# First four weight units loaded and converted along attention steps 28 to 84, in rooms of their own

## The chip, the cores and the metric

One core of one Trainium2 chip. The time is that of one execution on the device, in microseconds (us); of several runs the median is given. TensorE is called PE, VectorE DVE, ScalarE ACT, GpSimd POOL; SP issues the transfers.

## What is computed

Attention with two mixings over heads (2 batches, 12 heads, 448 rows, head size 64), then two dense blocks on the 896 rows of width 768. The reference, cut:

```python
scores = scale * q @ k.T
scores = einsum("bhij,hg->bgij", scores, w_pre)      # mix the heads
attn = softmax(scores)                               # maximum, exp, sum
attn = einsum("bhij,hg->bgij", attn, w_post)         # mix again
x = attn @ v                                         # rows of 768
xn = x / sqrt(mean(x * x) + 1e-6) * rms_g
y = (silu(xn @ w_gate) * (xn @ w_val)) @ w_out       # 768 -> 1536 -> 768
out = elu(y @ w_in) @ w_out2                         # 768 -> 2048 -> 768
```

The weights of the dense blocks arrive as 64-bit floats.

## The kernel before

**Weight units.** The weights are cut into units of 128 x 768 numbers. Units 0 to 23 are w_gate and w_val in turn, 0.77 MB each. `load_w` (L206) brings one into the tile raw (two rooms). `convert` (L214) makes it usable in stages: rebase (ACT L229 reads the high words into w32, DVE L232 shifts the low words), sign (DVE L237 clips and finds the largest number of each row, DVE L245 sets the sign), join (DVE L251 puts both words together and, for every second unit, L270 prepares the pair's largest numbers). For a pair of such units bound (PE L277) and factor (DVE L284, L288, L290) make a scale; then scaled (six ACT L301), high16 (ACT L305) and low16 (DVE L309) split the unit in two 16-bit halves in a tile whl (three rooms). `load_to(n)` issues all loads below n; `next_convert` and `next_scaled` hand out the first and the second part of the stages.

**Attention.** `attention` (L370) first turns q and k of batch 0 and splits each in two parts (par). There are twelve such parts a batch, but nine rooms of their own; `parts_of` (L431) gives three of batch 0 the rooms of whl, and of batch 1 the rooms of raw to two and of whl to one. The scores are written to memory (s_d) and come back in groups of ten rows by twelve heads (sg). There are 90 groups, and the main loop (L834) works as a pipeline with one group a step: at step t PE mixes group t+1 (L544, or L547 to L549), DVE takes the maximum of group t (L556), ACT the exponential (L564), DVE makes the low part el of group t-2 (L602) and the high part eh of t-1 (L595, or ACT L593), PE mixes group t-3 again (L623, it reads eh and el), ACT copies it out (L635). Beside that hq holds the turning of batch 1's q and k and the score rows, some a step. After each window of some 60 to 70 rows the products with v run (L659) and a chain of ten small stages follows, one a step: L665 and squares on POOL, mean (L681), root (POOL L692), diagonal (L696), spread (PE L702), normed (L705), high (ACT L711), low (L714) into xhl, which the dense blocks read.

**What sets the order.** All is recorded by hand in program order; each engine works in that order. In the loop one entry of the list tail is taken at the end of a step when hq is empty: load units 0 and 1, convert unit 0, load 2, convert 1, load 3, scale 0, scale 1. From the last step on `fill` also takes products of the first two units on batch 0's rows (`first_gate`, 12 pieces of three products) between the chain's stages, and with each an entry of more: convert units 2 and 3, load 4 and 5, scale 2. `run` (L909) then works unit by unit: unit 0 on batch 1's rows begins with the first L202 that reads the last window's xhl, and for u = 0 it also scales unit 3.

In this section step t is the t-th of the 90 rows of L556, counted from 0.

## Time and profile before

| | us |
|---|---|
| median of 3 runs | 782.35 (781.74 to 783.04) |
| the profiled execution | 782.59, its span 780.9 |
| PE busy | 747.8 (96%) |
| DVE busy | 552.1 (71%) |
| ACT busy | 438.5 (56%) |
| POOL busy | 94.6 (12%) |
| L556 of steps 28, 60, 67, 74, 84 | at 109.26, 191.53, 209.80, 227.25, 255.28 |
| first L202 on the last window's rows | at 292.58 |

How to read it: up to some 80 us attention starts up; from there to 270 us the 90 steps run; the dense blocks follow and fill PE to the end. The busy share of PE says where it waits for others, and the granted clock how fast it ran: 1.00 stands for 2.4 GHz, and the other level is 1.2 GHz. An idle DVE or ACT costs nothing unless PE waits for it in the end.

### The profile page before, as it was taken

Reading aid. Unit: us, or ns where it says so; the run is one execution under the profiler, and the core shown is the slowest. Engines: PE = TensorE matmul, PEld = TensorE weight load, DVE = VectorE, ACT = ScalarE, POOL = GpSimd, SP = SyncE. Lnnn points to the kernel's source line nnn. Section 1 sums busy time; section 2 is a strip of 40 time slices with the busy share of each in tenths; the row PEclk is TensorE's granted clock in tenths of the full one; section 3 lists DMA queues with packets and bytes.
Section 4 is the critical chain, followed back from the end, with each engine's and each line's share of the span. In section 5 each row is a group of like instructions: output and inputs, shape, how many; then the busy total and the mean of one; then the engine's idle time right before and its main releaser. Section 6 shows DMA issues by size and latency. Waiting matters only on the chain.

```text
span 780.9 us, 14563 instructions
## 1 busy us (share of the span) xinstructions
PE 747.8 (96%) x5683; PEld 590.3 (76%) x5683; DVE 552.1 (71%) x1101; ACT 438.5 (56%) x910; POOL 94.6 (12%) x117
## 2 busy tenths in 40 slices
PE   7789999999998879999999999999999999999996
PEld 5446787777776654555555589999999999999996
DVE  4358997788899867878878766653888788643731
ACT  3478788878777845666576622322776665221310
POOL 0122344334445300000000000000000000000000
PEclk8689999999999999999999999999999999999999
DMA  8698965668675023333333223322444244442602
GB/s 186 202 298 263 188 142 147 186 177 251 188 200 156 3 84 122 99 112 114 122 122 119 83 83 122 122 81 72 131 122 119 87 119 120 124 121 79 174 22 71
DMA packets 92873, 104.05 MB, mean 133 GB/s; under 512 B 21316, under 2 KB 88708, under 8 KB 92804
## 3 DMA queue, kind: packets, MB, share of 16 engines
q1 hardware_dynamic: 92804, 103.12, 46.8%
q8 instruction: 45, 0.74, 0.4%
q14 instruction: 24, 0.20, 0.1%
HBM read 81.08 MB, written 22.02 MB: 132 GB/s over the span
## 4 chain that ended last, share of the span: by engine, by line
PE 82%; DVE 6%; DMA 5%; ACT 3%; SPq 2%; issue 1%; POOL 1%; ACTq 0%; POOLq 0%; DVEq 0%
PE psa_t L202 12%; PE psa_t L204 12%; PE psa_t L203 12%; PE psv_t L659 4%; PE pst_t L623 4%; PE psa_t L1081 4%; PE psa_t L1079 4%; PE psa_t L1080 4%; PE psf_t L204 3%; PE psf_t L202 3%; PE psf_t L203 3%; PE psa_t L544 3%; PE psa_t L469 3%; DMA s_d<-st 2%; PE psf_t L1079 1%; PE psf_t L1080 1%
## 5 line engine op out<-in xcount | busy, mean ns | idle before, releaser
L257 ACT ACTIVATE whl<-w 128x768 fp32r<-128x768 f32 x44 | 37.2, 846 | 100.0 <-DVE w L251 47.9
L623 PEld LDWEIGHTS <-eh 120*112 120x112 f16 x720 | 66.0, 130 | 24.4 <-issue 17.2
L261 DVE TENSOR_TENSOR whl<-w,whl 128x768 fp32r<-128x768 f32 x44 | 42.2, 958 | 59.5 <-ACT whl L257 59.5
L229 ACT ACTIVATE w<-raw 128x768 f32<-128x768 f32 x68 | 61.7, 907 | 20.9 <-DVE whl L309 18.9
L537 POOL TENSOR_TENSOR sl<-sg,sh 120x448 fp32r<-120x448 f32 (+1 forms) x45 | 57.0, 1266 | 115.2 <-ACT sh L536 112.5
L204 PE MATMUL psa_t<-x2h,whl 128*128 128x448 f32 x192 | 70.5, 367 | 0.0
L202 PE MATMUL psa_t<-x2h,whl 128*128 128x448 f32 x192 | 70.1, 365 | 0.0
L203 PE MATMUL psa_t<-x2l,whl 128*128 128x448 f32 x192 | 69.9, 364 | 0.0
L564 ACT ACTIVATE e<-psa_t,nmax 120x448 f32<-120x448 f32 (+1 forms) x90 | 57.4, 638 | 20.9 <-DVE rs L579 17.8
L623 PE MATMUL pst_t<-m2h,el 120*112 120x120 f16 x360 | 62.3, 217 | 5.6 <-DVE el L602 5.6
L251 DVE SCALAR_TENSOR_TENSOR w<-w,raw 128x768 int32<-128x768 int32 x68 | 65.2, 959 | 1.1
L602 DVE SCALAR_TENSOR_TENSOR el<-e,rs,eh 120x448 f16<-120x448 f32 (+1 forms) x90 | 65.6, 728 | 0.0
L245 DVE SCALAR_TENSOR_TENSOR raw<-raw 128x768 int32<-128x768 int32 x68 | 64.8, 953 | 0.0
L623 PE MATMUL pst_t<-m2h,eh 120*112 120x120 f16 x360 | 62.3, 216 | 0.2 <-DVE el L602 0.2
L623 PE MATMUL pst_t<-m2l,eh 120*112 120x120 f16 x360 | 62.3, 216 | 0.0
L556 DVE TENSOR_REDUCE nmax<-psa_t 120x1 f32<-120x448 f32 (+1 forms) x90 | 55.0, 611 | 9.1 <-PE psa_t L549 9.0
L301 ACT ACTIVATE w<-w,gs 128x128 f32<-128x128 f32 x144 | 44.5, 389 | 26.7 <-DVE gs L290 26.7
L202 PE MATMUL psa_t<-xhl,whl 128*128 128x448 f16 x150 | 53.6, 357 | 3.5 <-ACT xhl L711 3.5
L659 PE MATMUL psv_t<-at,vs 112*64 112x70 f32 (+3 forms) x1344 | 55.7, 230 | 0.3 <-DVE sm L572 0.3
L1080 PE MATMUL psa_t<-whl,gh 128*128 128x384 f32 x160 | 54.1, 338 | 0.0
L1081 PE MATMUL psa_t<-whl,gl 128*128 128x384 f32 x160 | 54.1, 338 | 0.0
L1079 PE MATMUL psa_t<-whl,gh 128*128 128x384 f32 x160 | 54.1, 338 | 0.0
(160 smaller groups left out, 1891.7 us busy)
## 6 DMA issues: line engine op xcount, KB each, us to landing
raw<-in_moe_w_out_dram SPq DMA_DIRECT2D x28, 768.0 KB, 4.5
sg<-s_d SPq DMA_DIRECT2D x44, 420.0 KB, 5.1
s_d<-st SPq DMA_DIRECT2D x93, 196.0 KB, 3.0
raw<-in_moe_w_in_dram SPq DMA_DIRECT2D x16, 768.0 KB, 4.7
raw<-in_moe_w_gate_dram SPq DMA_DIRECT2D x12, 768.0 KB, 4.4
raw<-in_moe_w_val_dram SPq DMA_DIRECT2D x12, 768.0 KB, 4.5
vs<-in_v_dram SPq DMA_DIRECT2D x12, 224.0 KB, 6.1
qk<-in_k_dram SPq DMA_DIRECT2D x6, 224.0 KB, 4.8
```

The lines of the kernel that those rows point to most:

```text
L202: nc.tensor.matmul(out=ps, lhsT=wh(kk), rhs=xh_(kk), start=(first and kk == 0), stop=False)
L203: nc.tensor.matmul(out=ps, lhsT=wh(kk), rhs=xl_(kk), start=False, stop=False)
L204: nc.tensor.matmul(out=ps, lhsT=wl(kk), rhs=xh_(kk), start=False, stop=(last and kk == nk - 1))
L229: nc.scalar.activation(out=w, in_=raw.bitcast(F32)[:, :, 1], func=ACTF.Abs if small else ACTF.Copy, scale=REBASE)
L245: nc.vector.scalar_tensor_tensor(out=lo, in0=hi, scalar=SIGN, in1=lo, op0=ALU.bitwise_and, op1=ALU.bitwise_or)
L251: nc.vector.scalar_tensor_tensor(out=wi, in0=wi, scalar=3, in1=lo, op0=ALU.logical_shift_left, op1=ALU.bitwise_or)
L602: nc.vector.scalar_tensor_tensor(out=el[:r], in0=e32[:r], scalar=rs[:r], in1=eh[:r], op0=ALU.mult, op1=ALU.subtract)
L623: nc.tensor.matmul(out=o, lhsT=lhs[:r, c * CP:(c + 1) * CP], rhs=rhs[:r, :, :ni], start=(n == 0), stop=(n == 2),)
L659: nc.tensor.matmul(out=psx[s * D:(s + 1) * D, kk, :n], lhsT=vs[b, kk][:, s, c, :], rhs=at[:, c, hh, :n], start=(c == 0), stop=(c == NCH - 1),)
L1079: nc.tensor.matmul(out=o, lhsT=gh[:, kk, tk], rhs=wh[:, j], start=first, stop=False)
L1080: nc.tensor.matmul(out=o, lhsT=gh[:, kk, tk], rhs=wl[:, j], start=False, stop=False)
L1081: nc.tensor.matmul(out=o, lhsT=gl[:, kk, tk], rhs=wh[:, j], start=False, stop=end)
```

## The change

The first four units get a list tail of 43 entries (load, convert two units, scale both, twice over), which is spread evenly over steps 28 to 84 by a pace of 43/56 entries a step, whether hq is empty or not. The list more is gone, and `run` no longer scales unit 3. q and k have twelve rooms par of their own and no longer take those of raw and whl; whl has four rooms. The three tiles of the first mixing (m1f, m1h, m1l) move to the pool of attention, which ends with it. By the formula the conversion stages of the units fall to steps 34, 35 and 37 (unit 0), 41 to 43 (unit 1), 60, 61 and 63 (unit 2), 67 to 69 (unit 3), and the scalings to 47 to 51, 55 to 57, 73 to 77 and 81 to 83; the loads stand at steps 29 (two), 38, 44, 64 and 70. Numbers of lines in the new kernel are smaller by 3 in `convert` and by 10 in the attention's steps.

```diff
             )
 
         def high():
-            st["p"] = whl = wpool.tile([P, 2, n], F32R, tag="whl", name="whl", bufs=3)
+            st["p"] = whl = wpool.tile([P, 2, n], F32R, tag="whl", name="whl", bufs=4)
             nc.scalar.activation(out=whl[:, 0], in_=st["w"], func=ACTF.Copy)
 
         def low():
...
                 nc.scalar.activation(out=w, in_=w, func=ACTF.Copy, scale=grow[u][:, kk:kk + 1])
 
         def high16():
-            st["p"] = whl = wpool.tile([P, 2, n], F16, tag="whl", name="whl16", bufs=3, padded_shape=[P, 4, n])
+            st["p"] = whl = wpool.tile([P, 2, n], F16, tag="whl", name="whl16", bufs=4, padded_shape=[P, 4, n])
             nc.scalar.activation(out=whl[:, 0], in_=st["w"], func=ACTF.Copy)
 
         def low16():
...
 
             i = 2 * p + (tag == "qt")
             if (b, i) not in par:
-                own = ["par"] * 9 + ["whl"] * 3 if b == 0 else ["raw"] * 2 + ["par"] * 9 + ["whl"]
-                if own[i] == "par":
-                    t = ap.tile([P, 2, S], F32R, tag="par", name="par", bufs=9)
-                else:
-                    n = 3 if own[i] == "whl" else 2
-                    t = wpool.tile([P, 2 * KD * P], F32R, tag=own[i], name="par_" + own[i][0], bufs=n)
-                    t = t[:, :2 * S].rearrange("p (t s) -> p t s", t=2)
-                par[b, i] = t
+                par[b, i] = ap.tile([P, 2, S], F32R, tag="par", name="par", bufs=2 * NP)
             return [par[b, i][:, j] for j in range(2)]
 
         def turned(b, p, tag):
...
             return [lambda p=p: scores(b, p, c) for p in range(NP)]
 
         MIX = 3
-        mix = mixing()
+        m1f = ap.tile([GP, GP], F32, tag="m1f", name="m1f", bufs=1)
+        m1h = ap.tile([GP, GP], F32R, tag="m1h", name="m1h", bufs=1)
+        m1l = ap.tile([GP, GP], F32R, tag="m1l", name="m1l", bufs=1)
+        mix = mixing(m1f, m1h, m1l)
         load_first()
         warm()
         q_beside(0)
...
             if 0 <= t < n:
                 fn(*seq[t])
 
-        EARLY_GATES, GAP, FILL, END = 2, 2, 1, 1
+        EARLY_GATES, UNITS, BEGIN, END_AT, GAP, FILL, END = 2, 4, 28, 84, 2, 1, 1
         conv_now = []
 
         def pops(k):
...
             return [lambda: conv_now.extend(next_scaled(len(units)))] + [pops(2)] + [pops(1)] * 3
 
         tail = [lambda: load_to(2)] + [lambda: None] * 2
-        tail += unit() + [lambda: load_to(3)] + unit() + [lambda: load_to(4)] + scaling() + scaling()
-        more = unit() + [lambda: load_to(5)] + unit() + [lambda: load_to(6)] + scaling()
-
+        for j in range(0, UNITS, 2):
+            for i in range(2):
+                tail += unit() + [lambda n=j + i + 3: load_to(n)]
+            tail += scaling() + scaling()
+
+        pace = len(tail) / (END_AT - BEGIN)
         gates = []
 
         def fill(k):
...
                     gates.extend(first_gate(j))
             for _ in range(min(k, len(gates))):
                 gates.pop(0)()
-            if more:
-                more.pop(0)()
 
         for t in range(-6, n + 5):
             while v_next:
...
             while hq and popped < done:
                 hq.pop(0)()
                 popped += 1
-            if not hq and not on_act and not on_dve and tail:
-                tail.pop(0)()
+            for _ in range(int((t + 1 - BEGIN) * pace) - int((t - BEGIN) * pace) if t >= BEGIN else 0):
+                if tail:
+                    tail.pop(0)()
             step_chains()
             for _ in range(2 if t >= n else 1):
                 if wq:
...
             step_chains()
             fill(END)
         fill(len(gates))
-        while more:
-            more.pop(0)()
 
     with ExitStack() as actx:
         attention(actx)
...
         load_to(begun[0] + 2)
         v = begun[0]
         conv = []
-        rest = next_scaled(u + 3 if u == 0 else u + 2)
+        rest = next_scaled(u + 2)
         if v < len(units) and v <= u + (4 if units[v][4] else 2):
             conv = next_convert()
         conv = conv + [None] * (5 - len(conv))
```

DVE at step 61, before: eh of a group, then the window's products L705 and L665, then the next step's maximum and el (the number behind e_ names the group's buffer).

```order
L595 TENSOR_SCALAR eh<-e_3434,rs 120x448
L705 TENSOR_TENSOR xt<-xt,psa_t 128x6x58
L665 TENSOR_TENSOR xt<-psv_t,vsc 128x420
L572 TENSOR_SCALAR sm<-sm 120x1
L556 TENSOR_REDUCE nmax<-psa_t 120x1
L579 RECIPROCAL rs<-sm 120x1
L602 SCALAR_TENSOR_TENSOR el<-e_3434,rs,eh 120x448
L595 TENSOR_SCALAR eh<-e_3478,rs 120x448
```

The same place now, with the rebase of unit 2 a step ahead and its sign stage:

```order
L229 TENSOR_SCALAR raw<-raw 128x768
L562 TENSOR_SCALAR sm<-sm 120x1
L546 TENSOR_REDUCE nmax<-psa_t 120x1
L569 RECIPROCAL rs<-sm 120x1
L592 SCALAR_TENSOR_TENSOR el<-e_3414,rs,eh 120x448
L585 TENSOR_SCALAR eh<-e_3483,rs 120x448
L234 TENSOR_SCALAR w_3499,wm<-w_3499 128x768
L242 SCALAR_TENSOR_TENSOR raw<-raw 128x768
L695 TENSOR_TENSOR xt<-xt,psa_t 128x6x58
L655 TENSOR_TENSOR xt<-psv_t,vsc 128x420
L562 TENSOR_SCALAR sm<-sm 120x1
L546 TENSOR_REDUCE nmax<-psa_t 120x1
```

L229, L234 and L242 (L232, L237 and L245 of before) are new there; clip and sign stand in front of the window's two products.

DVE at the end of attention, before, from the join of unit 3 to the last low part of xhl (psw is the room of the last windows' small products):

```order
L251 SCALAR_TENSOR_TENSOR w_4979<-w_4979,raw 128x768
L270 TENSOR_SCALAR wm<-wm 128x2
L705 TENSOR_TENSOR xt<-xt,psw_t 128x6x60
L688 TENSOR_SCALAR ms<-psw_t 48x1
L284 TENSOR_SCALAR inv<-psa_t 128x2
L288 RECIPROCAL up<-inv 128x2
L290 TENSOR_TENSOR gs<-g_dn,up 128x12
L714 TENSOR_TENSOR xhl<-xt,xhl 128x6x60
L696 TENSOR_SCALAR dg<-ident,rstd 48x48
L309 TENSOR_TENSOR whl_5066<-w_4858,whl_5066 128x768
L705 TENSOR_TENSOR xt<-xt,psw_t 128x6x48
L714 TENSOR_TENSOR xhl<-xt,xhl 128x6x48
```

The same place now:

```order
L655 TENSOR_TENSOR xt<-psv_t,vsc 128x6x48
L695 TENSOR_TENSOR xt<-xt,psw_t 128x6x60
L678 TENSOR_SCALAR ms<-psw_t 48x1
L704 TENSOR_TENSOR xhl<-xt,xhl 128x6x60
L686 TENSOR_SCALAR dg<-ident,rstd 48x48
L695 TENSOR_TENSOR xt<-xt,psw_t 128x6x48
L704 TENSOR_TENSOR xhl<-xt,xhl 128x6x48
```

The join, the bound's factors and the low16 of unit 2 are gone from between the window's stages; no stage of the window has moved against another.

SP at step 29, before: the last loads of q and k, then groups and stores of score rows.

```order
L392 DMA kt<-in_k_dram 112x8x64
L392 DMA qt<-in_q_dram 112x8x64
L508 DMA sg<-s_d_91 120x2x448 x3
L488 DMA s_d_92<-st 112x448 x2
```

And now:

```order
L389 DMA kt<-in_k_dram 112x8x64
L389 DMA qt<-in_q_dram 112x8x64
L498 DMA sg<-s_d_88 120x2x448
L205 DMA raw<-in_moe_w_gate_dram 128x6x256
L205 DMA raw<-in_moe_w_val_dram 128x6x256
L498 DMA sg<-s_d_88 120x2x448 x2
L478 DMA s_d_89<-st 112x448 x2
```

Two loads of weight units stand between two group loads; the other loads follow alone in the same manner.

## Rows read from the trace of the kernel before

**Rows 1.** Stretches: start and end, length, then busy by engine, clock, DMA, GB/s.

```profile
80.00:108.00 28.00, 27.57 (x377) 22.56 (x376) 27.01 (x73) 22.66 (x55) 12.43 (x17) 1.00 0.88 175
108.00:228.00 120.00, 119.37 (x1570) 92.94 (x1569) 101.44 (x267) 96.39 (x233) 48.83 (x59) 1.00 0.67 182
228.00:264.00 36.00, 31.70 (x421) 25.16 (x420) 33.80 (x84) 26.10 (x62) 15.79 (x16) 0.95 0.49 134
264.00:280.00 16.00, 13.33 (x233) 10.50 (x233) 13.67 (x32) 11.86 (x27) 3.51 (x6) 1.00 0.07 16
280.00:292.58 12.58, 7.69 (x99) 4.85 (x95) 6.35 (x18) 4.15 (x11) 0.54 (x1) 0.87 0.32 110
292.58:300.00 7.42, 7.42 (x30) 3.34 (x30) 4.69 (x8) 4.13 (x9) 0.00 (x0) 0.76 0.33 103
```

**Rows 2.** Timeline of PE: start, duration, instruction, idle time before and releaser.

```profile
199.73 0.26 PE L623 MATMUL pst_t<-m2h,el 120*112 120x120 f16 x1
...
218.94 0.22 PE L623 MATMUL pst_t<-m2h,el 120*112 120x120 f16 x1
...
236.07 0.26 PE L623 MATMUL pst_t<-m2h,el 120*112 120x120 f16 x1 [2.70 <-DVE el L602]
...
237.88 0.29 PE L681 MATMUL psa_t<-ones,sq 128*70 128x2 f32 x2 [1.08 <-POOL sq L675]
...
288.67 0.39 PE L702 MATMUL psw_t<-dg,ones 48*128 48x48 f32 x2 [1.37 <-DVE dg L696]
...
292.58 0.53 PE L202 MATMUL psa_t<-xhl,whl 128*128 128x448 f16 x1 [3.52 <-ACT xhl L711]
```

**Rows 3.** Timeline of DVE, the same columns.

```profile
198.81 0.86 DVE L602 SCALAR_TENSOR_TENSOR el<-e,rs,eh 120x448 f16<-120x448 f32 x1
...
215.56 0.86 DVE L602 SCALAR_TENSOR_TENSOR el<-e,rs,eh 120x448 f16<-120x448 f32 x1
...
231.67 0.94 DVE L237 TENSOR_SCALAR_CACHE_REDUCE w<-w 128x768 f32<-128x768 f32 x1
...
232.54 1.03 DVE L245 SCALAR_TENSOR_TENSOR raw<-raw 128x768 int32<-128x768 int32 x1
...
287.37 0.16 DVE L284 TENSOR_SCALAR inv<-psa_t 128x2 f32<-128x2 f32 x1 [1.12 <-PE psa_t L277]
...
290.73 0.96 DVE L309 TENSOR_TENSOR whl<-w,whl 128x768 f16<-128x768 f32 x1 [2.21 <-ACT whl L305]
...
291.61 0.45 DVE L705 TENSOR_TENSOR xt<-xt,psw_t 128x288 f32<-128x288 f32 x1
```

**Rows 4.** DVE groups, 215 to 300 us: busy us, mean ns, idle before.

```profile
L251 DVE SCALAR_TENSOR_TENSOR w<-w,raw 128x768 int32<-128x768 int32 x5 | 5.1, 1019 | 0.0
...
L245 DVE SCALAR_TENSOR_TENSOR raw<-raw 128x768 int32<-128x768 int32 x5 | 4.8, 965 | 0.0
...
L237 DVE TENSOR_SCALAR_CACHE_REDUCE w<-w 128x768 f32<-128x768 f32 x5 | 4.7, 939 | 0.0
...
L309 DVE TENSOR_TENSOR whl<-w,whl 128x768 f16<-128x768 f32 x4 | 3.8, 956 | 6.5 <-ACT whl L305 6.5
...
L232 DVE TENSOR_SCALAR raw<-raw 128x768 int32<-128x768 int32 x6 | 3.3, 554 | 0.7 <-DMA raw<-in_moe_w_gate_dram 0.7
...
L270 DVE TENSOR_SCALAR wm<-wm 128x2 int32<-128x2 int32 x2 | 1.3, 632 | 0.0
```

**Rows 5.** ACT groups of the same stretch.

```profile
L301 ACT ACTIVATE w<-w,gs 128x128 f32<-128x128 f32 x24 | 7.4, 388 | 1.8 <-DVE gs L290 1.8
...
L229 ACT ACTIVATE w<-raw 128x768 f32<-128x768 f32 x6 | 5.4, 906 | 0.9 <-DMA raw<-in_moe_w_gate_dram 0.9
...
L305 ACT ACTIVATE whl<-w 128x768 f16<-128x768 f32 x4 | 3.4, 842 | 3.0 <-PE psa_t L204 3.0
```

**Rows 6.** Who waited for whom, 108 to 228 us: total, times, longest.

```profile
DVE sm L572 <- ACT e L564: 18.5, 20, 4.1
```

**Rows 7.** Timeline of POOL at 248 us.

```profile
247.89 3.02 POOL L537 TENSOR_TENSOR sl<-sg,sh 120x448 fp32r<-120x448 f32 x1 [2.90 <-ACT sh L536]
```

More of the change, by code (lines that the diff above doesn't have):

```diff
@@ L112, in block_kernel @@
     g_top = const.tile([P, P], BF16, name="g_top")
-    m1f = const.tile([GP, GP], F32, name="m1f")
-    m1h = const.tile([GP, GP], F32R, name="m1h")
-    m1l = const.tile([GP, GP], F32R, name="m1l")
     m2h = const.tile([GP, H, GI], F16, name="m2h")
@@ L125, in load_small, with mixing @@
         )
-    def mixing():
+    def mixing(m1f, m1h, m1l):
         selr, cmax, rcm, m2p = slot(H, GI, H), slot(P, H), slot(P, H), slot(GP, H, GI)
```

## The prediction

> **What bounds the kernel now.** I read the busy time by stretches first, to see where TensorE (PE) is not full. From 108 to 228 us (steps 28 to about 74 of attention) PE is busy 119.37 of 120 us at clock 1.00: this stretch is bound by PE, while VectorE (DVE) has 18.6 us free and ScalarE (ACT) 23.6 [rows 1]. From 228 to 292.58 us PE idles 4.30, 2.67 and 4.89 us in three stretches, and the granted clock falls to 0.95 and, after the last pause, to 0.76 [rows 1]; later stretches are full. So all that this change can win lies between 228 and 300 us, and the place where it puts the work is one in which any delay of DVE that reaches PE is lost time.
>
> Then the order of time, to see what PE waits for. At 236.07 it has waited 2.70 us for el, which DVE makes, and at 237.88 another 1.08 for the squares; at 288.67 it waits 1.37 for the diagonal and at 292.58 it waits 3.52 for the last window's xh, on which the first gate product of the second half hangs [rows 2]. DVE's rows at those times show why: the clip and the sign operation of unit 0 (L237, L245) fill 231.67 to 233.6, just ahead of the el that PE lacks; at the end DVE sits 1.12 us until PE has done the bound of units 2 and 3 (L284), then 2.21 us until ACT has rounded unit 2 (L309), and only then does the normalisation L705 of the last window come, at 291.61 [rows 3]. DVE works in order, so a waiting conversion holds up the window behind it.
>
> **What goes.** Four terms, each from the idle time of its stretch.
> (1) 228 to 264 us, idle 4.30. Units 0 and 1 leave it: per unit L232 0.55, L237 0.94, L245 0.97, L251 1.02 = 3.48 us of DVE, and L270 0.63 each [rows 4], so 8.2 us of DVE; the two low16 (L309, 0.96 each) of units 2 and 3 come in. DVE falls from 33.80 to about 27.5 of 36 us, and PE becomes the late one. I take the 4.30 as won and nothing for the clock's 5% (1.8 us), since a stall elsewhere can bring that back.
> (2) 264 to 280 us, idle 2.67. Two L309 and unit 2's conversion go, 2 x 0.96 + 3.48 = 5.4 us of DVE's 13.67; what stays is the latency of the last groups. I take 2.0.
> (3) 280 to 292.58 us, idle 4.89. Between the diagonal's product (L702) and the first gate product there must remain L705 on DVE and L711 on ACT with their hops: from L705's start at 291.61 to PE at 292.58 are 0.97 us [rows 2, 3], with the hop ahead of it some 1.1. So 3.8 goes.
> (4) 292.58 to 300 us at clock 0.76: 0.24 x 7.42 = 1.8 us. In 264 to 280 us, where PE paused by shorter pieces, the clock stayed at 1.00 [rows 1], so with a pause of 1.1 I take all of it.
> Sum: 4.3 + 2.0 + 3.8 + 1.8 = 11.9 us. Bounds: 8 if term (1) gives only a tenth of its idle time, because the steps behind 74 still carry two scalings on ACT (six L301 and L305 each); 14.4 with the clock of (1) and all of (2).
>
> **What comes.** Into 108 to 228 us go all four conversions, and the scaling of units 0 and 1. DVE: 4 x 3.48 + 2 x 0.96 + 2 x 0.63 = 17.1 us; ACT: 4 x 0.91 (L229) + 2 x 1.85 (L301, 7.4 us over four units) + 2 x 0.84 (L305) = 9.0 us [rows 4, 5]. ACT has 23.6 us free for it, but six L301 in a row stand ahead of the next exponential and can delay it by 1.85 us at two places. DVE would be busy 101.44 + 17.1 = 118.5 of 120 us. No row shows DVE as full as that, so I bound the stretching by the two fullest ones: 27.01 of 28 us (96.5%) in 80 to 108, with PE hardly idle, and 33.80 of 36 (93.9%) in 228 to 264, with PE waiting [rows 1]. 118.5 / 0.965 = 122.8 and 118.5 / 0.939 = 126.2, so the cost is 2.8 to 6.2 us. It is not zero, although 18.6 us are free, because the free time is mostly one wait (18.5 us in 20 pieces for ACT's exponential [rows 6]), which lies where it lies and not where the table puts a unit. How much delay PE stands is the distance from an el's end to its use: 2.5 us at step 67 (215.56 + 0.86 against 218.94), but 0.06 us at step 60 (198.81 + 0.86 against 199.73) [rows 2, 3]. Unit 2's clip and sign operation, 1.9 us, now stand just there, ahead of the same pair L705 and L665 as unit 0's before; units 3's stand so at step 68. Units 0 and 1 come where DVE has more gaps. So I take 5.0, above the middle.
>
> Four more things cost nothing by this trace. The bound's product (L277) and its factors only move. The loads: four of 0.77 MB now pass SP's queue among the loads of score groups, 3.1 MB beside the 182 GB/s x 120 us = 21.8 MB that run there at a share of 0.67 [rows 1]; each is issued five steps or more ahead of its use, and they stand no nearer to a group's load than the first pair did before. If that fails, ACT waits for a late group and PE two steps later. The own rooms for q and k: a buffer's last reader (the scores of chunk 3) stands ahead of the new transposes on PE in both versions, so nothing waits less or more. The fourth room for finished units: ACT no longer waits for unit 0's last product before it rounds unit 3, but PE was full by then.
>
> **A rule against the change.** At 247.89 POOL's subtraction took 3.02 us, where POOL's mean is 48.83 / 59 = 0.83, and L270, on 256 numbers, has a mean of 0.63 us where L284 on as many took 0.16 [rows 1, 3, 4, 7]. The Trainium skill, SBUF — State Buffer, section SBUF: two separate sides, says that VectorE and GpSimd share one pair of ports, and that a VectorE operation with two SBUF inputs and a GpSimd operation that reads SBUF lock each other out for a whole instruction. These two rows agree. By that rule, as an estimate from this page and POOL's rows (busy 48.8 of 120 us, against 4.1 of 28.6 behind 264), the six two-input operations of units 2 and 3 would meet POOL 27% more often, each for about half of 0.83 us: 0.7 us more, so 776.2 instead of the number below.
>
> **Sum.** The profiled execution took 782.59 us, 1.7 above its span of 780.9 and 0.24 above the median of 782.35. 782.6 - 11.9 + 5.0 = 775.7; against the median 775.5.
>
> **Rivals.**
> (A) The free time takes everything: DVE's 18.6 us free against 17.1 added. Then nothing is lost in the loop, and 11.9 to 14.4 us are won: 768 to 770.5. For it: 80 to 108 us has DVE at 96.5% and PE nearly full. Against it: the 0.06 us at step 60. Chance 0.12.
> (B) Slower: each unit costs what unit 0 costs now, a PE wait of 2.70 and 1.08 us [rows 2] and the clock's 1.8 behind it, 5.6 us; four of them are 22.4, and 782.35 - 11.9 + 22.4 = 792.9. The mechanism is the sign stage (two DVE operations at once) ahead of a window's two products, at a step in which el has no lead. It turns the sign of the result from 3.0 us a unit on (11.9 / 4). Against it: two of the four units have gaps around them, and unit 1 now costs no such wait. Chance 0.09.
> (C) The bound takes DVE's lead: L284 must wait until PE, which is up to 2.5 us behind, has done L277; at the end of the kernel before this wait was 1.12 us [rows 3]. Two pairs, each losing the whole lead: 5 us more, 780.5. Against it: at the first place (step 47) DVE is stopped by ACT anyway. Chance 0.07.
> (D) Won and lost come out even, 781 to 784: the 8 of the low bound against 6.2 and one clock drop of 1.8. Chance 0.06.
>
> **How the numbers follow.** The forecast, 771 to 780.5, has 0.66: its ends are 782.35 - 14.4 + 2.8 = 770.8 and 782.35 - 8.0 + 6.2 = 780.5. The range 770.0 to 781.5 leaves out most of (A), half of (D) and all of (B), about 0.2. A measurement of this kernel can tell about 0.2% (1.6 us) from no change: below 780.8 is faster. Faster: 0.66 + 0.12 + 0.03 of (C) = 0.81; same: the rest of (C) and (D) = 0.10; slower 0.09.
>
> **What would show it.** Right: PE idle under 1.5 us between the last premix and the last window's wait, that wait near 1.1 us and clock 1.00 behind it; DVE at 96% or more in steps 28 to 74, this stretch some 5 us longer, with PE waits for el at steps 61 to 63 and 69 to 71. Wrong: waits of 2 us and more at all four units and a clock under 1.00 in the loop (B), waits of L284 on L277 of 2 us (C), or a wait for a score group's load, which I hold for covered.

## The result

The changed kernel takes 772.55 us (median of 4 runs, 771.71 to 774.99), the kernel before 782.33 on the same chip (4 runs, 781.74 to 783.04): ratio 0.988, 95% interval 0.9855 to 0.9904. That is 9.8 us less, where 6.9 were forecast, and inside the range of 770.0 to 781.5. In a later comparison on another occasion it took 775.18 against 783.21, ratio 0.99 (0.9877 to 0.9924): 8.0 us. So it is faster, and the forecast was right in sign and size. In part that is luck. More was paid in the loop than I had forecast (8.0 us in the first profile, 7.0 in a repeat, against 5.0) and a little more was won behind it (12.5 against 11.9), so by the forecast's own terms 4.5 us should have been left; the rest of the gain came from places that the forecast does not name (see the section on why it was right).

The page of the profiled execution (774.99 us, 1.7 above its span, and the slowest of the four), the rows that answer to those of before; the slices of the clock are a fortieth of the span each:

```profile
span 773.3 us, 14550 instructions
...
PE 747.1 (97%) x5683; PEld 587.9 (76%) x5683; DVE 550.3 (71%) x1101; ACT 436.7 (56%) x910; POOL 97.6 (13%) x117
...
PEclk9679999999999999999999999999999999999999
```

To compare stages I cut both traces at the same work: the maximum of step 28, of step 74, of step 89, the first product of the second half's gate, the end of SP's last issue of an output transfer. In this order the kernel before took 117.99, 39.78, 25.55 and 485.59 us from mark to mark, the changed kernel 125.98, 34.13, 20.19 and 483.49. Step 28 itself came at 109.3 and at 106.8 us. The changed kernel by stretches (start and end, length, busy by engine, clock, DMA, GB/s): steps 28 to 74, steps 74 to 89, from there to the gate product, and the 7.4 us behind it:

```profile
106.80:232.78 125.98, 121.11 (x1549) 93.13 (x1546) 112.63 (x293) 102.77 (x248) 52.95 (x58) 0.99 0.72 201
232.78:266.91 34.13, 32.47 (x436) 25.77 (x435) 31.20 (x83) 28.93 (x73) 13.70 (x16) 0.95 0.32 78
266.91:287.10 20.19, 18.95 (x310) 14.10 (x309) 8.90 (x25) 6.95 (x16) 4.04 (x7) 1.00 0.01 3
287.10:294.50 7.40, 7.25 (x38) 3.69 (x38) 6.84 (x12) 1.52 (x2) 0.00 (x0) 1.00 0.31 103
```

And of the kernel before, cut at the same work:

```profile
109.30:227.29 117.99, 117.36 (x1546) 91.51 (x1541) 99.43 (x263) 95.45 (x230) 47.81 (x58) 1.00 0.66 181
...
227.29:267.07 39.78, 34.52 (x445) 26.90 (x445) 37.59 (x96) 28.60 (x68) 15.79 (x16) 0.96 0.47 128
267.07:292.58 25.51, 18.91 (x304) 13.88 (x302) 16.95 (x41) 13.57 (x32) 4.05 (x7) 0.94 0.20 65
```

Three things are to be read here. Behind step 74 PE idled 5.3 and 6.6 us in the kernel before, and 1.7 and 1.2 in the changed one: that is the gain. Ahead of step 74 PE idled 0.6 us before and 4.9 after, and DVE is no fuller than 112.63 of 125.98 us, 89%: that is the price, and DVE did not have to run full for it. (The idle time accounts for 4.3 of the 8.0 us. The rest is time in which PE is listed as busy, 121.11 us against 117.36 for nearly as many products; up to 1.7 of it is a fall of the clock, told in the last section, and no row shows the remainder.) And the clock behind the gate product is 1.00 where it was 0.76 [rows 1], with 38 products in 7.4 us instead of 30.

The end of attention is now what the forecast described. PE waits 0.21 and 1.02 us there, where it waited 1.37 and 3.52 [rows 2] (PE's timeline: start, duration, instruction, idle time before and releaser):

```profile
285.67 0.39 PE L692 MATMUL psw_t<-dg,ones 48*128 48x48 f32 x2 [0.21 <-DVE dg L686]
287.07 0.35 PE L199 MATMUL psa_t<-xhl,whl 128*128 128x448 f16 x1 [1.02 <-ACT xhl L701]
```

On DVE no conversion stands between the diagonal and the normalisation of the last window any more; the next one (L229) comes behind the window's last operation:

```profile
285.28 0.24 DVE L686 TENSOR_SCALAR dg<-ident,rstd 48x48 f32<-48x48 f32 x1 [0.44 <-POOL rstd L682]
286.09 0.46 DVE L695 TENSOR_TENSOR xt<-xt,psw_t 128x288 f32<-128x288 f32 x1 [0.57 <-PE psw_t L692]
287.06 0.46 DVE L704 TENSOR_TENSOR xhl<-xt,xhl 128x288 f16<-128x288 f32 x1 [0.51 <-ACT xhl L701]
287.43 0.56 DVE L229 TENSOR_SCALAR raw<-raw 128x768 int32<-128x768 int32 x1
```

In the loop PE has waits that were not there before; of its six rows only the last, with 0.5 us, stood there before too (who waited for whom, 106.8 to 232.78 us: total, times, longest):

```profile
PE psa_t L459 <- ACT e L554: 1.1, 1, 1.1
PE pst_t L613 <- DVE el L592: 1.0, 1, 1.0
PE psa_t L534 <- ACT e L554: 0.8, 2, 0.6
PE psa_t L537 <- ACT e L554: 0.6, 1, 0.6
PE psv_t L649 <- DVE sm L562: 0.5, 1, 0.5
PE psa_t L671 <- POOL sq L665: 0.5, 1, 0.5
...
DVE sm L562 <- ACT e L554: 13.2, 14, 2.5
...
ACT e L554 <- DVE rs L569: 12.1, 11, 2.6
```

The forecast looked for el; of 4.5 us listed, el is 1.0 and a late exponential is 2.5 (PE cannot begin scores or a premix while ACT has not read the accumulator it needs). DVE's wait for the exponential fell from 18.5 [rows 6] to 13.2 us, and ACT's exponential now waits 12.1 us for DVE, where it waited 7.1 before (109.3 to 227.29 us; the list names rs, which follows the maximum on DVE):

```profile
ACT e L564 <- DVE rs L579: 7.1, 10, 1.7
```

In both loops the wait for the exponential is the only one that DVE has: 99.43 us of work and 18.5 of this wait make 117.9 of 117.99 us before, 112.63 and 13.2 make 125.8 of 125.98 now.

### The profile page after: what moved, and what is told of

Read it like the earlier page. It is cut to its first block, busy times and chain, and to the rows that moved or that the text cites. A ratio compares the mean times of both kernels' runs of the same rounds, so it can differ in the third digit from the quotient of the medians.

```text
span 773.3 us, 14550 instructions
## 1 busy us (share of the span) xinstructions
PE 747.1 (97%) x5683; PEld 587.9 (76%) x5683; DVE 550.3 (71%) x1101; ACT 436.7 (56%) x910; POOL 97.6 (13%) x117
## 4 chain that ended last, share of the span: by engine, by line
PE 78%; DVE 7%; DMA 6%; ACT 5%; issue 2%; SPq 1%; POOL 0%; POOLq 0%; ACTq 0%; DVEq 0%
PE psa_t L200 12%; PE psa_t L199 12%; PE psa_t L201 12%; PE pst_t L613 4%; PE psv_t L649 4%; PE psa_t L1074 4%; PE psa_t L1072 3%; PE psa_t L1073 3%; PE psf_t L200 3%; PE psf_t L199 3%; PE psf_t L201 3%; DMA s_d<-st 3%; PE psa_t L534 3%; PE psa_t L459 2%; DVE nmax L546 2%
## 5 line engine op out<-in xcount | busy, mean ns | idle before, releaser
L226 ACT ACTIVATE w<-raw 128x768 f32<-128x768 f32 x68 | 61.6, 908 | 25.6 <-DVE whl L306 18.9
L248 DVE SCALAR_TENSOR_TENSOR w<-w,raw 128x768 int32<-128x768 int32 x68 | 65.2, 959 | 1.1
L242 DVE SCALAR_TENSOR_TENSOR raw<-raw 128x768 int32<-128x768 int32 x68 | 65.1, 958 | 0.0
L625 ACT ACTIVATE at<-pst_t 112x480 f32<-112x480 f32 (+1 forms) x90 | 52.6, 585 | 3.7 <-PE pst_t L613 3.3
```

The lines of the kernel that those rows point to most:

```text
L226: nc.scalar.activation(out=w, in_=raw.bitcast(F32)[:, :, 1], func=ACTF.Abs if small else ACTF.Copy, scale=REBASE)
L242: nc.vector.scalar_tensor_tensor(out=lo, in0=hi, scalar=SIGN, in1=lo, op0=ALU.bitwise_and, op1=ALU.bitwise_or)
L248: nc.vector.scalar_tensor_tensor(out=wi, in0=wi, scalar=3, in1=lo, op0=ALU.logical_shift_left, op1=ALU.bitwise_or)
```

## The experiments

**The rooms alone.** The rooms of q and k, whl and the first mixing as in the changed kernel, the order of the work as in the kernel before.

```diff
-        EARLY_GATES, UNITS, BEGIN, END_AT, GAP, FILL, END = 2, 4, 28, 84, 2, 1, 1
+        EARLY_GATES, GAP, FILL, END = 2, 2, 1, 1
...
-            for _ in range(int((t + 1 - BEGIN) * pace) - int((t - BEGIN) * pace) if t >= BEGIN else 0):
-                if tail:
-                    tail.pop(0)()
+            if not hq and not on_act and not on_dve and tail:
+                tail.pop(0)()
```

> Own rooms for q and k, four rooms for finished units, and the first mixing's tiles moved, but the conversions stay where they were before. Theory 1 (all of the gain comes from where the conversions stand; the 2.5 us by which the traced run after reached step 28 earlier are chance): 782.3, within 1 us. Theory 2 (the rooms themselves shorten the start): 779.8, with step 28 near 106.8 us instead of 109.3.

780.38 us, ratio 0.997 (0.9947 to 0.9992): a small gain where the first theory expected none. The number is nearer the second theory's 779.8, but its mechanism did not show: step 28 came at 108.7 us, not at 106.8. Its stages are 118.00, 40.89 and 25.56 us, within 1.2 us those of the kernel before; the pause at the gate product is again 3.52 us, the clock behind it 0.73. So the rooms change nothing in attention. The gain lies some 160 us and more behind the gate product, where PE waits for nothing in either kernel and its products simply follow each other a little faster (last section).

**No work for the first four units**, once in the changed kernel and once in the kernel before: the bounds, the conversions and the scalings of units 0 to 3 are left out, and constants, which POOL writes at steps 76, 78 and 80 and behind attention, stand for their finished values; the loads stay.

```diff
-            return [lambda: conv_now.extend(next_convert())] + [pops(1)] * 3
+            return [lambda: None] * 4
...
-            return [lambda: conv_now.extend(next_scaled(len(units)))] + [pops(2)] + [pops(1)] * 3
+            return [lambda: None] * 5
```

> The changed kernel without the work of the first four units (left out: rebase to low16 of units 0 to 3; their finished tiles are filled with a constant by POOL at steps 76, 78, 80 and behind attention; the loads stay). It prices the new place. Theory 1: steps 28 to 74 lose the 8.0 us that the trace after shows more there, so 764.5, and 767.5 if the forecast's 5.0 was right. Rival A (the free time of DVE takes it all): 771 to 772.5.

> The same leaving out (units 0 to 3 filled with a constant at the same places) in the kernel before. It prices the old place. Theory 1: the rooms do nothing, so it ends where the changed kernel without that work ends, 764.5 within 1.5 us, and the old place costs 18 us, of which the two late scalings stay after the change. Theory 2: it stays 2.5 us behind the other.

768.27 and 766.83 us, ratios 0.9828 (0.9803 to 0.9853) and 0.9804 (0.978 to 0.9828): without the work the two kernels are nearly alike, as they should be, and both are slower than the 764.5 expected. By these times the work cost 15 us at its old place (0.0196 of 783), and 4 to 6 us at its new one (0.988 to 0.99 against 0.9828). The traces put the new price higher: from step 28 to the gate product the changed kernel takes 180.3 us (179.3 in its repeat) and 171.0 without the work, so 8 to 9 us; but it reaches step 28 at 106.8 us, and the run without the work only at 110.6, which makes up for 3.8 of them. At the old place the same stretch takes 183.3 us with the work and 170.7 without, 12.7 us, and 1.5 more go to the clock behind it. The loop of the first run shows the price from the inside: steps 28 to 74 take 118.05 us, PE and DVE as in the kernel before, and the wait of DVE for the exponential is back at 18.5 us in 20 pieces. The loads stand in this loop as well, so it is not they that cost. Its row:

```profile
110.60:228.65 118.05, 117.40 (x1548) 91.44 (x1543) 99.47 (x263) 95.52 (x230) 47.62 (x58) 1.00 0.76 213
```

**Clip and sign operation one entry apart**, so that a unit never puts two operations of 0.95 us on DVE in one step.

```diff
-            return [rebase, sign, join, high, low]
+            return [rebase, both, join, high, low]
...
+            if apart:
+                stages = [stages[0], *halves[u], stages[2]]
...
-            return [lambda: conv_now.extend(next_convert())] + [pops(1)] * 3
+            return [lambda: conv_now.extend(next_convert(True))] + [pops(1)] * 4
```

> The changed kernel with clip and sign operation of a unit one table entry apart, 47 entries instead of 43 over the same steps 28 to 84. If the cost in the loop is the burst of two DVE operations of 0.95 us in one step: 2 us less, 770.5. If it is only DVE's sum, or ACT: 772.5 within 0.7.

774.99 us, ratio 0.9905 (0.9879 to 0.9932): not told apart from the changed kernel, where 2 us less were expected if the burst is what costs. Steps 28 to 74 take 124.18 us, 0.8 less than the better of two profiles of the changed kernel (next run). So the burst is not the cause, at most 0.8 us of it.

**The changed kernel once more**, **one step more of lead**, **no scaling**, and **three steps later**. Lead: postmix, output and windows one step later, eh and el with a room more, xt with two rooms instead of three (the rooms are left out of the cut below). No scaling: of the four units only load and conversion are left, without bound, factors, scaling, rounding and remainder. The last two have one run each, 773.41 and 772.15 us.

> The changed kernel once more, unaltered, as the measure for the three others. Theory: the 118.0 and 126.0 us that steps 28 to 74 took in the kernel before and in the changed one are properties of the order of work, so this run shows 126.0 again within 0.2; the time at which step 28 comes (106.8 to 110.8 us so far) is chance of the first 50 us and may be anywhere in that span; from the first gate product of the second half to the end about 482.5. Rival: the 126.0 was itself a chance of one execution, then it differs by more than 1 us. Time 771 to 775.

```diff
-            at_step(g_out, t - 4)
+            at_step(g_out, t - 5)
...
-            at_step(g_postmix, t - 3)
+            at_step(g_postmix, t - 4)
```

> As the changed kernel, but the product behind the softmax (postmix), its output and the windows' start come one step later, with one more room each for eh and el (and two instead of three for xt): el and the sums have 2.6 us more of lead. Theory 1 (PE loses the 8.0 us of steps 28 to 74 because el and sm come too late for it): the waits for el and for sm at the postmix go, steps 28 to 74 fall from 126.0 to 121 or less, the end of attention pays about 1 us for the extra step, the time falls by about 4 us. Rival (what is late is the exponential, which holds the accumulators that the next premix needs, so the lead of el does not matter): steps 28 to 74 stay above 124.5, and the time is equal or 1 us longer.

```diff
             return [lambda: conv_now.extend(next_convert())] + [pops(1)] * 3
...
-            return [lambda: conv_now.extend(next_scaled(len(units)))] + [pops(2)] + [pops(1)] * 3
+            return [lambda: None] * 5
```

> As the changed kernel, but of the first four weight units only the load and the conversion (rebase, clip, sign, join) are done in the steps; the bound, the factors, the scaling on ScalarE, the rounding and the remainder of all four are left out, and constants stand in for their values. Theory 1 (DVE's conversion of a unit, 3.5 us at one place, is what PE pays for): steps 28 to 74 stay at 124 to 125.5, since the delay against the kernel before grew by 2.9, 2.8 and about 2.4 us at units 1, 2 and 3 and by 0.7 at the two scalings together. Rival (six ACT scalings of 0.3 us in a row hold up the exponential and with it PE's accumulators): most of the 8.0 us goes, 118 to 121.

```diff
-        EARLY_GATES, UNITS, BEGIN, END_AT, GAP, FILL, END = 2, 4, 28, 84, 2, 1, 1
+        EARLY_GATES, UNITS, BEGIN, END_AT, GAP, FILL, END = 2, 4, 31, 87, 2, 1, 1
```

> As the changed kernel, with the same work spread over steps 31 to 87 instead of 28 to 84, so that each stage meets another phase of the windows (which come every 6 or 7 steps). Theory 1 (a unit costs PE time where its clip and sign operation stand ahead of a window's products, and nothing in a gap): the losses move, unit 0 now costs 1 us or more, one of the others costs nothing, and the total of steps 28 to 74 differs from 126.0 by more than 1 us. Rival (DVE has become full: every unit costs about the same wherever it is): 125 to 126, only 0.5 to 1 less because unit 3's last stages fall behind step 74.

The repeat: steps 28 to 74 in 124.95 us, 1.0 less than in the first profile, against an expected 0.2, so one execution says no more than about 1 us. PE's waits are the same within 0.5 us; what differs is the clock, of which the last section tells.

```profile
106.80:231.75 124.95, 119.64 (x1549) 92.20 (x1546) 112.72 (x294) 102.96 (x248) 52.55 (x58) 1.00 0.73 203
```

The lead: 124.71 us in the loop and 779.0 in all (ratio 0.994, 0.9917 to 0.9963). The wait for el is gone, as wanted, and PE waits elsewhere instead, for an accumulator that DVE's normalisation still reads (behind the loop the lead costs more than the 1 us expected: the stage ahead of the gate product takes 22.87 us, not 20.19):

```profile
PE psa_t L459 <- DVE xt L695: 2.5, 2, 1.4
PE psa_t L671 <- POOL sq L665: 1.1, 2, 0.7
PE psa_t L537 <- ACT e L554: 1.0, 2, 0.7
```

So my theory that the short distance from el to its product is what costs PE falls (the missing room of xt shows no wait on DVE in this loop). Without the scaling the loop takes 124.88 us, of which a fall of the clock is up to 1.7 (0.83 in ten microseconds): the scaling on ACT is not the cause, at most 1 to 2 us of it. Three steps later the loop takes 124.33 us; the delay against the kernel before, counted from step 28, is smaller behind unit 1 (1.4 us at step 48 instead of 3.1 to 3.7), and the sum is hardly smaller.

**DVE and ACT waiting in turn.** The traces suggested another theory. In step 43 of the changed kernel DVE reaches the maximum only after the join of unit 1, the shift of the pair's largest numbers and a window's normalisation (DVE's timeline):

```profile
147.36 0.61 DVE L546 TENSOR_REDUCE nmax<-psa_t 120x1 f32<-120x448 f32 x1
...
149.25 1.04 DVE L248 SCALAR_TENSOR_TENSOR w<-w,raw 128x768 int32<-128x768 int32 x1
150.21 0.27 DVE L267 TENSOR_SCALAR wm<-wm 128x2 int32<-128x2 int32 x1
150.40 0.52 DVE L695 TENSOR_TENSOR xt<-xt,psa_t 128x360 f32<-128x360 f32 x1
...
150.90 0.61 DVE L546 TENSOR_REDUCE nmax<-psa_t 96x1 f32<-96x448 f32 x1
...
155.70 0.15 DVE L562 TENSOR_SCALAR sm<-sm 120x1 f32<-120x1 f32 x1 [1.13 <-ACT e L554]
```

ACT sits idle 2.41 us until that maximum is there; then all its copies stand in a row ahead of the next exponential, so DVE waits 1.13 us at 155.70:

```profile
151.60 0.63 ACT L554 ACTIVATE e<-psa_t,nmax 96x448 f32<-96x448 f32 x1 [2.41 <-DVE rs L569]
...
154.94 0.63 ACT L554 ACTIVATE e<-psa_t,nmax 120x448 f32<-120x448 f32 x1
```

Three runs test it: the maximum ahead of the sum, the exponential ahead of ACT's split, and the first exchange in the kernel before.

```diff
-            at_step(g_sum, t - 1)
             at_step(g_max, t)
+            at_step(g_sum, t - 1)
```

> As the changed kernel, with two DVE instructions exchanged in every step: the maximum of step t (which releases the exponential of step t on ACT) now stands ahead of the sum of step t-1 (which waits for the exponential of step t-1). Theory 2: the spread work costs 7 to 8 us because DVE and ACT wait for each other in turn. In the repeated run of the changed kernel DVE's work in steps 28 to 74 is 112.7 us and its waits for the exponential are 12.1 us in 14 pieces, together 124.8 of the 124.9 us of this stage, and ACT's exponential waits 12.1 us for DVE. The exchange gives the exponential up to 0.53 us more of lead at each of the 14 places: about 7 us less, a stage of 118 to 121, the total 4 to 7 us shorter, 768 to 771. Rival (the units' DVE work itself is what PE pays for, wherever ACT stands): 124 to 125 as before. Rival 2: DVE now waits for PE's premix instead, stage of 126 or more.

```diff
-            at_step(g_split, t + 3)
             at_step(g_exp, t)
+            at_step(g_split, t + 3)
```

> As the changed kernel, with two ACT instructions exchanged in every second step: the exponential now stands ahead of the split of a score group (0.57 us, issued 0.46 us apart). Theory 2 (DVE waits for an exponential that stands behind ACT's copies): at up to 14 waits, half of them in such steps, the exponential comes 0.46 us earlier, the stage of steps 28 to 74 falls by 1 to 3 us to 122 to 124. Rival (the place of ACT's copies does not matter, DVE's own work sets the stage): 124.5 to 126.

> The kernel before with the exchange of the maximum and the sum alone, as the control: there PE is busy 117.3 of 117.9 us in steps 28 to 74, so DVE's waits of 18.5 us cost nothing in this stage. Theory 2: this stage stays at 118.0, DVE's waits fall all the same; steps 74 to 89, in which unit 0 and 1 stand, may gain 1 to 3 us; total 779 to 782. Rival (the exchange is good or bad for every step by itself): this stage changes by over 1 us.

The first: 779.05 us, 0.9948 (0.9924 to 0.9971). That is 8 us and more above the expected 768 to 771. DVE's wait for the exponential fell to 4.1 us, as the theory says, and yet the loop became longer, 129.03 us (up to 3.4 of it a low clock, 0.91 and 0.75 in two stretches of ten microseconds). DVE now waits for PE, as the second rival had it, the exponential waits longer for DVE than in the changed kernel, and DVE's own busy time grew from 112.7 to 118.4 us (110.9 to 239.93 us):

```profile
DVE sm L562 <- ACT e L554: 4.1, 7, 1.0
DVE nmax L546 <- PE psa_t L534: 1.9, 4, 1.1
DVE nmax L546 <- PE psa_t L539: 1.4, 1, 1.4
DVE inv L281 <- PE psa_t L274: 1.3, 1, 1.3
...
ACT e L554 <- DVE sm L562: 16.6, 13, 2.5
```

The second: 779.25 us, 0.9967 (0.9941 to 0.9992), loop 125.82. The wait fell to 8.5 us, and DVE's busy time rose from 112.7 to 116.1 instead: el became longer by more than eh became shorter (DVE groups of the loop, count, busy, mean ns; this run, then the changed kernel's repeat):

```profile
L592 DVE SCALAR_TENSOR_TENSOR el<-e,rs,eh 120x448 f16<-120x448 f32 (+1 forms) x46 | 41.3, 897 | 0.0
...
L585 DVE TENSOR_SCALAR eh<-e,rs 120x448 f16<-120x448 f32 (+1 forms) x38 | 18.2, 479 | 0.0
```

```profile
L592 DVE SCALAR_TENSOR_TENSOR el<-e,rs,eh 120x448 f16<-120x448 f32 (+1 forms) x46 | 33.8, 735 | 0.0
...
L585 DVE TENSOR_SCALAR eh<-e,rs 120x448 f16<-120x448 f32 (+1 forms) x38 | 22.1, 581 | 0.0
```

The split's place decides when POOL's subtraction runs. Of the 45 el of 120 rows in this loop, 18 overlap it and take 1158 ns on average, the other 27 take 702; no eh overlaps it. In the changed kernel's repeat 13 el (855 ns, the others 689) and 8 eh (896 ns, the others 499) do. So el takes 46 x 0.162 = 7.5 us more and eh 3.9 less. The Trainium skill, SBUF — State Buffer, section SBUF: two separate sides, says that an operation of VectorE with two SBUF inputs, as el is, and a GpSimd one that reads SBUF shut each other out; this trace agrees, with 1158 ns for an el that meets the subtraction and 702 for one that does not. The control: loop 116.79 us (1.2 less, 0 expected), steps 74 to 89 in 42.52 instead of 39.78, 785.48 us in all, 1.0041 (1.0022 to 1.0061). It is a little worse, and the gain that I expected behind the loop did not show (the clock was 0.88 in that stage, against 0.96 in the kernel before, which is up to 3.4 us of it). The theory falls in its simple form: to shorten that one wait gives nothing, since another engine's wait, or more of DVE's own time, takes its place.

**Each stage in a step of its own.** The last theory was of place: sign stages stood in steps 42, 61 and 68, with a window's wide DVE operations, and there the delay grew by 2.5 to 3 us in the first profile (by 1 to 2 at unit 2 in the repeat, where the clock did not fall there).

```diff
-            for _ in range(int((t + 1 - BEGIN) * pace) - int((t - BEGIN) * pace) if t >= BEGIN else 0):
-                if tail:
-                    tail.pop(0)()
+            while tail and tail[0][0] <= t:
+                tail.pop(0)[1]()
...
+        STEPS = [
+            28, 31, 33, 34, 38, 38, 40, 41, 44, 46, 46, 47, 48, 49, 50, 50, 51, 52,
+            53, 56, 58, 62, 62, 69, 71, 72, 74, 74, 76, 77, 78, 79, 80, 81, 83,
+        ]
```

> As the changed kernel, but every stage of the four units has a step of its own by a table: the clip and the sign operation apart, and each DVE operation of a conversion in a step in which no window has one of its wide DVE operations (squares, normalisation, remainder). In the changed kernel the sign stage of unit 1 stands in step 42 with a window's squares and its join in step 43 with a normalisation, and the sign stages of units 2 and 3 in steps 61 and 68, each with both; there the delay against the kernel before grows by 2.5 to 3 us each, while unit 0 in steps 34 to 37 costs nothing for good. Unit 3's conversion moves to steps 69 to 74. Theory 3 (a unit costs PE time where two wide DVE additions meet in one step): the jumps of 2 to 3 us go, steps 28 to 74 take 119 to 122, the total is 766 to 770. Rival (the amount of DVE work in the stage sets the loss, 7 us for 15 us of work, wherever it stands): with one unit's sign and join work at its end the stage still takes 123 to 125, the total is 771 to 775.

775.28 us, 0.9895 (0.9872 to 0.9918): the changed kernel's time, where 766 to 770 were expected. The loop takes 125.96 us, of which up to 1.7 is again a fall of the clock. The jumps are gone, as the theory wanted: the largest growth in two steps is 1.8 us. But the same delay comes in small steps, 0.8 at step 40, 1.6 at 46, 3.2 at 52, 5.5 at 62, 8.0 at 74. The theory of place falls too:

```profile
108.40:234.36 125.96, 120.99 (x1558) 93.16 (x1555) 111.77 (x288) 103.29 (x248) 48.33 (x58) 0.99 0.73 201
```

What stands: six orders of the same work (as changed, sign apart, later, placed, with more lead, with the exponential ahead) have a loop of 124.2 to 125.8 us once the falls of the clock are taken out; the exchange of maximum and sum comes to the same 125.6. The price is 6 to 8 us for some 13 us that DVE is busier (112.72 against 99.43), about half a microsecond for each, hardly moved by the order. What stays open is why it is just a half, and whether DVE's work alone sets it: ACT is busier too (102.77 against 95.45 us), and each unit's conversion on ACT (L226, 0.9 us) stood in all these versions. It is not one wait: each one that I took away came back on another engine or as DVE's own time. Runs with half or double the DVE work, at an unchanged order, or with ACT's part of the conversion left out, would tell; they were not made. No version beats the changed kernel by what the times can tell: the one three steps later had one run of 772.15 and is not told apart from it. (In the traces sign apart and three later are shorter from step 28 to the gate product, 177.8 and 176.8 us against 180.3 and 179.3.)

## Why the prediction was right, point by point

Terms (1) to (3), the gain ahead of the gate product: 10.1 us were forecast; measured were 39.78 - 34.13 = 5.65 and 25.55 - 20.19 = 5.36, together 11.0. The remaining pause of 1.1 came out as 1.02, and from the last premix to its end PE idled 1.23 us, where under 1.5 was the sign of being right.

Term (4), the clock behind the pause, 1.8 us: the rows show 0.76 before and 1.00 after. Counted in products from the first one of the gate, the tenth behind it comes at 3.69 us before, 2.20 after and 3.81 with the rooms alone, where pause and clock are the old ones; and the last product of the kernel comes 482.00 and 480.52 us behind the first. So the term was 1.5. (The other 0.6 of this stage lies behind the last product.)

The cost in the loop is the term that was mis-sized: 5.0 us forecast, within 2.8 to 6.2; measured 8.0, and 7.0 in the repeat. The step that failed is the bound by DVE's fill. It let DVE go to 94 or 96.5%, after rows of other stages; in the loop DVE stopped at 89 to 90%. A second error hid part of this one: 17.1 us of work were added to DVE's busy time, which rose by only 13.2 (99.43 to 112.63). The conversions' own operations did come to 18.4 us, but eh fell from a mean of 646 to 581 ns (2.5 us over 38), the low parts xhl by 1.0 us, and operations that follow each other overlap in the list (the sum of all durations rose by 15.7). With the measured 112.63 us the same bound would have given 117 to 120 us, which is hardly any cost; that it came within 2 to 3 us of the measured cost is luck. The 18.6 us of free time were seen rightly as one wait that lies where it lies [rows 6], and the conclusion was too mild: of those 18.5 us only 5 to 6 could be filled. That units 0 and 1 come where DVE has more gaps held for unit 0 (no delay is left at step 41) and not for unit 1 (2.5 us at steps 42 to 44). The forecast of PE waits for el at steps 61 to 63 came true once, with 0.99 us at 201.62; at step 69 it was the exponential, 1.1 us, and a wait for el came at step 77 instead.

The total: -11.0 - 1.5 + 8.0 = -4.5 us by the forecast's own terms, where -6.9 is on record. Of the 7.6 us between the two spans the rest is 0.6 at the very end and 2.5 by which step 28 comes earlier, 106.8 against 109.3 us. That is ahead of all moved work; it lies between 106.8 and 110.8 us in the kernels with an unchanged beginning, whichever tail they have, and 29 runs of the kernel before spread from 779.4 to 785.7. What sets the time of step 28 no run shows. That it is the chance of one execution is not likely, since the repeat of the changed kernel came to step 28 at 106.8 us again; and the change did not aim at it, since the same beginning with the rooms alone came there at 108.7. So these 2.5 us, without which the first profile would show 5.1, are luck as far as the forecast goes, and the repeat's 8.0 is as good a figure as 9.8.

The rivals. (A), that the free time takes it all, would have left the loop at 118 us. (B) had 5.6 us a unit; measured were 7.0 / 4 = 1.8 in the repeat. (C), the bound's factors waiting for PE: there is no such row in the loop of the changed kernel; the wait does appear where the order is another (1.3 us with the maximum first, above). (D), no change, was not met. The rule on the shared port was weighed at 0.7 us, for the conversions' own two-input operations. These grew by little: over the four units of the loop L242 has a mean of 1022 ns and L248 of 1024, against 965 and 1019 [rows 4], 0.25 us in all. POOL became busier in the loop, 52.95 against 47.81 us for the same 58 instructions, and el went from a mean of 720 to 735 ns, 0.7 us over 46 of them, while eh became shorter by the 2.5 us named above. All of this is within what the times can't tell.

## What to carry to other kernels

Free time of an engine that is one half of a ring (DVE waits for ACT's exponential, which waits for DVE's maximum, and PE waits for both) is not free: here about a third of it could be filled, and the rest was paid by the engine that sets the pace. Work that stands ahead of a dependent tail is still worth moving into such a loop: by the times 15 us at the tail became 4 to 6, by the traces 14 became 8 to 9. To size such a move, take the work out at both places first; two runs then give both prices, which no reading of fill gave here. Compare the stages as well as the times, since other parts of the kernel can shift by some microseconds meanwhile, as step 28 did here.

## What the runs showed of the chip

The clock fell after shorter pauses than I had thought, and not each time. In the changed kernel PE waited 0.99 us for el at 201.62 and 0.51 us at 202.86; before that the clock was 1.00, and behind it PE ran at 0.51, so at the lower level of 1.2 GHz, for some 3 us:

```profile
197.00:204.00 7.00, 5.40 (x74) 4.09 (x73) 7.00 (x17) 4.43 (x12) 3.73 (x6) 1.00 0.65 155
204.00:207.00 3.00, 3.00 (x23) 1.92 (x19) 3.00 (x9) 1.51 (x5) 2.13 (x1) 0.51 0.87 231
```

In the repeat of the same program the same two waits (0.98 and 0.51 us) left it at 1.00, with 48 products in the 3 us instead of 23:

```profile
197.00:204.00 7.00, 5.42 (x63) 4.03 (x63) 7.00 (x17) 4.44 (x12) 3.51 (x5) 1.00 0.62 144
204.00:207.00 3.00, 3.00 (x48) 2.19 (x44) 3.00 (x8) 1.94 (x6) 2.38 (x1) 1.00 0.91 250
```

This is where the two loops come to differ by 1.0 us. In four of the fourteen profiles (the changed kernel, without scaling, maximum first, placed) such waits in the loop were followed by 3 to 7 us at half clock, in others by none. A small wait of PE in a full loop may so cost more than its length, though no run shows that the waits are the cause, and two profiles of one program can differ by it.

The other surprise is the pace of products that wait for nothing. In the last part of the kernel PE is 100% busy at clock 1.00 in every kernel, with the same products; they take 338 ns in the kernel before and without the work, and 334 in the changed kernel and with the rooms alone (PE by groups, before and then changed):

```profile
L1079 PE MATMUL psa_t<-whl,gh 128*128 128x384 f32 x157 | 53.1, 338 | 0.0
```

```profile
L1072 PE MATMUL psa_t<-whl,gh 128*128 128x384 f32 x159 | 53.1, 334 | 0.0
```

The last 684 products take 120.53 us in the first two and 118.75 in the others. Of the thousand ahead of them it is not the same kernels that are fast: 203.55 before, 202.36 with the rooms alone, 205.33 in the changed kernel, and to 0.01 us the same in its repeat. So the pace belongs to the program, not to the execution. The other versions fall into such classes too: from the first gate product to the last it is 480.52 us in the changed kernel, its repeat, three later and placed, and 478.19 in sign apart, maximum first and exponential ahead, so their times as a whole can't be set against each other without these 2.3 us. Between the kernel before and the changed one it cancels by accident (324.08 and 324.09 us over both parts); the rooms alone win 2.8 us by it, which is their ratio of 0.997. What sets it (where the rooms lie, what the other engines do meanwhile, or something else) no run told apart.
